# Causal masks from TensorE to GpSimd, 14 and 6 products of P V in a PSUM tile, and the last tokens of two batches in one output chunk, with a new written order

## The chip, the cores and the metric

The kernel runs on one core of a Trainium2 chip, as one launch. The metric is the device time of one execution in microseconds. The time before is the median of three runs.

## What is computed

Attention with a forget gate for 8 batches of 8 heads (576 tokens, head size 64), and then a gated FFN with a convolution of three taps over the tokens:

```python
scores = scale * np.matmul(q, k.transpose(0, 1, 3, 2))
cum = np.cumsum(np.log(np.clip(f, 0.0001, 1.0)), axis=-1)
scores = np.where(causal, -1e9, scores + cum[:, :, :, None] - cum[:, :, None, :])
attn = softmax(scores)                       # over the keys
x = np.matmul(attn, v)                       # heads side by side: 576 x 512 for each batch
h = np.maximum(x @ w_in, 0.0)                # 512 -> 1024
conv = sum of conv_w[k] * h shifted by k - 1 # along the tokens
out = (h * sigmoid(conv)) @ w_out            # 1024 -> 512
```

Inputs and output are float32; the matmuls run in 16-bit types.

## The kernel before

**Work.** The 64 heads go in 16 half batches `hb` of four heads. 576 tokens are four blocks of 128 and a tail of 64. Scores are made transposed, keys on the partitions. For each pair of heads `i` (two pairs in a half batch) `sd` makes the diagonal blocks, `so` the blocks off the diagonal (one step for each head), and `st` the tail's own 64 x 64 blocks for the half batch. `ed`, `eo` and `et` are ScalarE's exponentials of these. The decay is in the scores' matmul already, through two more rows of K and Q.

**The mask.** For half batches in `MASK_PE` a matmul with the identity (`masked`, L370) adds -1e30 above the diagonal before the scores are added, and ScalarE writes the result in 16 bits. For the others `ed` and `et` write float32 tiles (`pd`, `p3`, two of each), and GpSimd's `md` and `mt` (L406, L385) select from these into the 16-bit tiles. `signs`, the constants for the decay rows, lie in one of the `pd` tiles.

**P V and its normalization.** `pv` (L438) multiplies the exponentials by V with a column of ones, 65 columns for each head and block of queries, in three steps for a half batch: query blocks 0 and 1, blocks 2 and 3, the tail. Each takes one PSUM tile. `n` on VectorE takes the reciprocal of the sums (L445) and multiplies (L446). `t` and `tx` turn the result for the FFN.

**The FFN.** For each batch `b` and each 128 columns `ff` of 1024: `f` (L468) on PE, `r` (relu, L478) on ScalarE, `c` and `d` (the convolution, L483 and L485) on VectorE, `a` (tanh, L488) on ScalarE, `g` (the gate, L492) on VectorE. The second matmul `o` goes by chunks of 128 tokens over all `ff` (L499); the tail of 64 tokens goes by itself, in two halves of 256 columns (L503). `e` evicts from PSUM and `s` stores. In the last batch these go chunk by chunk as gates get ready.

**Loads.** SyncE (SP) issues them in order: `ld` (plain loads of Q and K for the first two half batches, transposed on PE by `tp`), `q` (transposing loads, L229), `v`, the weights `wi` and `wo`, and the decay rows `rw` and `fi`, which come from an image in memory that `ki` and `zc` write. `cl` writes Q and K from PSUM (L221, L223) or clamps them after the transposing load (L235); `va` casts V (L266, L268) and `wic` and `woc` cast the weights (L546).

**The order.** `ORDER` is a list of about a thousand steps, written by a search. Each engine issues its steps in the order of that list, and `@` names the engine where there is a choice. Four PSUM tiles `ps` of 1024 float32 columns and the other buffers are given out in that order too.

## Time and profile before

| | |
|---|---|
| median of three runs | 256.92 us (256.37 to 257.09) |
| span of the profiled execution | 254.4 us |
| PE (matmuls) busy | 235.6 us, 93% of the span |
| DVE (VectorE) busy | 216.8 us, 85% |
| ACT (ScalarE) busy | 217.4 us, 85% |
| POOL (GpSimd) busy | 45.9 us, 18% |
| moved by DMA | 48.24 MB, 190 GB/s in the mean |

The profiled execution's own time is not listed beside its span. The span goes from its first to its last instruction; the three runs' times hold what lies around that as well. Busy times are sums over the span; an engine with less busy time than another can still set the pace in one stage. The granted clock of TensorE is 0.999 of full speed in the mean.

### The profile page before, as it was taken

The numbers are of one execution on the slowest core, as the hardware profiler recorded it, in microseconds if no ns is written. First come the engines' busy times: TensorE is split into PE (matmuls) and PEld (weight loads), VectorE is DVE, ScalarE is ACT, GpSimd is POOL, SyncE is SP. The second block draws the span as 40 slices with busy tenths as digits, with TensorE's granted clock in tenths as the row PEclk, the third lists the DMA queues.
The fourth block names the chain that finished last, engine by engine and source line by source line (L and its number), as shares of the span: only waits on it lengthen the run. The fifth ranks groups of instructions, "written<-read, shape, count | busy, mean of one in ns | idle before, by whom it ended". The sixth has DMA issues, their size and how long they took to land.

```text
span 254.4 us, 6767 instructions
## 1 busy us (share of the span) xinstructions
PE 235.6 (93%) x2784; PEld 171.8 (68%) x2784; DVE 216.8 (85%) x353; ACT 217.4 (85%) x295; POOL 45.9 (18%) x79
## 2 busy tenths in 40 slices
...
GB/s 181 304 163 225 225 208 172 196 198 293 210 193 207 260 124 230 213 253 208 212 259 247 200 179 213 230 238 174 223 236 270 251 23 80 5 84 1 103 112 180
DMA packets 114695, 48.24 MB, mean 190 GB/s; under 512 B 104034, under 2 KB 105250, under 8 KB 114664
## 3 DMA queue, kind: packets, MB, share of 16 engines
...
q0 software_dynamic: 208, 0.51, 0.6%
...
## 4 chain that ended last, share of the span: by engine, by line
PE 57%; DVE 15%; DMA 9%; SPq 7%; ACT 5%; issue 4%; POOL 0%; DVEq 0%; POOLq 0%; ACTq 0%
PE ps L468 14%; PE ps L499 14%; PE ps L362 12%; PE ps L438 9%; DVE u L483 5%; DVE hg L492 4%; SPq L258 4%; DMA vf<-in_v_dram 4%; DVE u L485 3%; DMA hg<-in_k_dram 3%; PE ps L454 2%; PE ps L503 2%; DMA qk<-in_k_dram 2%; ACT pp L420 2%; PE ps L370 2%
## 5 line engine op out<-in xcount | busy, mean ns | idle before, releaser
L420 ACT ACTIVATE pp<-ps 128x1024 f16<-128x1024 f32 x64 | 65.0, 1038 | 6.6 <-PE ps L362 4.9
L468 PE MATMUL ps<-xt,w_in_f 128*128 128x288 f16 x512 | 68.9, 286 | 1.8 <-ACT xt L459 0.8
L362 PE MATMUL ps<-qk 128*128 128x128 bf16 (+2 forms) x576 | 63.6, 240 | 1.6 <-ACT ht L478 1.1
L499 PE MATMUL ps<-w_out_f,hg 128*128 128x512 f16 x256 | 59.9, 379 | 0.1
L468 PEld LDWEIGHTS <-w_in_f 128*128 128x128 f16 x512 | 48.8, 98 | 15.8 <-issue 2.5
L483 DVE SCALAR_TENSOR_TENSOR u<-ht,cwt 128x576 f32<-128x576 f16 x64 | 54.8, 862 | 2.8 <-ACT ht L478 2.8
L485 DVE SCALAR_TENSOR_TENSOR u<-ht,cwt,u 128x576 f32<-128x576 f16 x64 | 52.9, 831 | 1.7
L362 PEld LDWEIGHTS <-qk 128*128 128x128 bf16 x576 | 40.7, 98 | 17.6 <-issue 3.6
L488 ACT ACTIVATE hg<-u,cw 128x576 f16<-128x576 f32 x64 | 49.0, 786 | 1.8 <-DVE u L485 1.5
L492 DVE SCALAR_TENSOR_TENSOR hg<-hg,ht 128x576 f16<-128x576 f16 x64 | 49.6, 804 | 0.8 <-ACT hg L488 0.8
L478 ACT ACTIVATE ht<-ps 128x576 f16<-128x576 f32 x64 | 41.2, 667 | 5.4 <-PE ps L468 4.6
L499 PEld LDWEIGHTS <-hg 128*128 128x128 f16 x256 | 24.2, 98 | 25.4 <-DVE hg L492 0.8
L438 PE MATMUL ps<-va,pp 128*128 128x65 f16 x896 | 33.5, 193 | 4.0 <-POOL va L266 1.8
L438 PEld LDWEIGHTS <-pp 128*128 128x128 f16 x896 | 32.1, 97 | 6.2 <-issue 3.2
L406 POOL TENSOR_SCALAR_AFFINE_SELECT pp<-pd 128x1024 f16<-128x1024 f32 x16 | 19.4, 1215 | 63.9 <-ACT pd L403 60.8
L446 DVE TENSOR_TENSOR xm<-ps,rc 128x512 f16<-128x512 f32 (+1 forms) x48 | 28.9, 603 | 1.7
L509 ACT COPY ob<-ps 128x1024 f32<-128x1024 f32 (+1 forms) x21 | 16.8, 800 | 2.4 <-PE ps L503 1.0
L403 ACT ACTIVATE pd<-ps 128x1024 f32<-128x1024 f32 x16 | 16.6, 1036 | 1.0 <-PE ps L362 0.8
L403 ACT ACTIVATE pp<-ps 128x1024 f16<-128x1024 f32 x16 | 16.2, 1038 | 1.3 <-PE ps L362 1.3
L235 DVE TENSOR_SCALAR qk<-qk,lim 128x2304 uint16<-128x2304 uint16 x12 | 10.4, 875 | 7.3 <-DMA qk<-in_k_dram 4.9
L370 PE MATMUL ps<-mask,ident 128*128 128x512 bf16 (+1 forms) x40 | 14.3, 358 | 0.7 <-ACT ht L478 0.4
L445 DVE RECIPROCAL rc<-ps 128x8 f32<-128x8 f32 (+1 forms) x48 | 9.3, 193 | 5.9 <-PE ps L438 4.9
...
## 6 DMA issues: line engine op xcount, KB each, us to landing
...
out_dram<-ob SPq DMA_DIRECT2D x14, 512.0 KB, 3.1
...
ob<-in_moe_w_in_dram SPq DMA_DIRECT2D x4, 512.0 KB, 5.8
ob<-in_moe_w_out_dram SPq DMA_DIRECT2D x4, 512.0 KB, 6.4
...
```

What stands on the lines that cost most here:

```text
L362: nc.tensor.matmul(o, tk[:, h * S + k0:h * S + k0 + 128], tq[:, h * S + q0:h * S + q0 + n], start=first, stop=last and not by_matmul(hb, h))
L403: nc.scalar.activation(o, ps_of(f"sd{i}").rearrange("p (s c) -> p s c", s=2), AF.Exp, scale=SCALE)
L420: nc.scalar.activation(pair(i)[:, s, 512:1536], ps_of(f"so{i}.{s}"), AF.Exp, scale=SCALE)
L438: nc.tensor.matmul(o, block(hb, h, m, n), va[:, h, m, 0:D + 1], start=(m == 0), stop=(m == n))
L446: nc.vector.tensor_tensor(xm[:, 2 * u:2 * u + nj, :].rearrange("p j (h d) -> p j h d", d=D), got[:, :, :, 0:D], r.unsqueeze(3).broadcast_t ...
L468: nc.tensor.matmul(ps[:, MB + 288 * a:MB + 288 * (a + 1)], w_in_f16[:, cc, 128 * ff:128 * (ff + 1)], xt[:, cc, 288 * a:288 * (a + 1)], sta ...
L478: nc.scalar.activation(ht_of(b, ff)[:, 1:1 + S], ps_of(f"f{b}.{ff}")[:, MB:MB + S], AF.Relu, scale=0.5)
L483: nc.vector.scalar_tensor_tensor(u, ht[:, 0:S], cwt[:, ff, 0:1], ht[:, 1:1 + S], op0=ALU.mult, op1=ALU.add)
L485: nc.vector.scalar_tensor_tensor(u, ht[:, 2:2 + S], cwt[:, ff, 1:2], u, op0=ALU.mult, op1=ALU.add)
L488: nc.scalar.activation(hg_of(b, ff), u_t[slot[f"c{b}.{ff}", "u"]], AF.Tanh, scale=cw[:, ff, 1:2])
L492: nc.vector.scalar_tensor_tensor(hv, hv, 1.0, ht_of(b, ff)[:, 1:1 + S], op0=ALU.add, op1=ALU.mult)
L499: nc.tensor.matmul(ps[:, 512 * (c % 2):512 * (c % 2 + 1)], hg_of(b, ff)[:, 128 * c:128 * (c + 1)], w_out_f16[:, ff, :], **kw)
```

## The change

Four things change in the code, and the order is a new one.

- The mask of half batches 2 to 7 is GpSimd's, as that of 8 to 15 is already. `signs` gets a tile of its own, since the `pd` tiles are now used earlier.
- P V of a half batch goes into two PSUM tiles instead of three: the first holds 14 products (query blocks 0 to 2 and two heads of block 3), seven to a bank, the second the other 6. Normalization has two steps.
- A new step `k` copies the last 64 tokens of each batch's gated columns into a tile `tl` that two batches share, batch by batch, and `ff` by `ff` in the last one. The second matmul runs over these 128 tokens once for two batches, with all 512 columns.
- In the new order, 12 diagonal and 6 tail masks, 18 casts of V and all 8 weight casts are GpSimd's (before: 8 casts of V and 6 of the weights), `ki` is on GpSimd's queue instead of SP's, and evictions and casts are spread anew over ScalarE and VectorE.

The start of both orders, and the code:

```diff
-cw dca ld0 ld0.1.1 dcl dcs ld0.0.0 ld1 ld0.0.1 tp0.0.0 cl0.0.0@ACT cwt ld0.1.0 tp0.0.1 tp0.1.0 tp0.1.1 ld1.0.0 tp1.0.0
-dck cl0.0.1@ACT cl0.1.0@DVE cl0.1.1@ACT cl1.0.0@ACT ld1.0.1 tp1.0.1 q2.0 cl2.0 cl1.0.1@ACT sd0 ed0 tp1.1.0 tp1.1.1
-cl1.1.1@ACT ki@SP q2.1 sd1 so0.0 eo0.0 ed1 so1.1 eo1.1 so1.0 v0.0 v0.3 cl1.1.0@DVE rw1 so0.1 eo1.0 eo0.1 v0.4 v0.2
-v0.1 sd3 ed3 so3.0 sd2 eo3.0 ed2 cl2.1 wi0 rw2 wi1 wic1@POOL so2.1 va1.0@DVE eo2.1 st0 et0 va0.0@DVE va0.1@DVE pv0.0
-n0.0 so2.0 st1 et1 eo2.0 pv0.1 so3.1 pv0.2 eo3.1 va1.1@ACT sd5 q3.1 n0.1 n0.2 pv1.0 q3.0 wi3 n1.0 pv1.1 n1.1 pv1.2
-n1.2 ed5 so5.1 eo5.1 cl3.1 wic0@POOL t0 tx0@ACT t1 tx1@DVE cl3.0 wi2 wic3@POOL q5.0 sd4 ed4 rw3 so4.1 eo4.1 f0.0 r0.0
-f0.1 f0.2 f0.3 q5.1 v1.0 r0.1 v1.1 v1.2 v1.3 va2.0@POOL c0.0 d0.0 c0.1 wic2@ACT q4.1 r0.3 d0.1 so4.0 f0.4 c0.3 r0.2
-c0.2 d0.3 eo4.0 h0 sd7 sd6 so5.0 a0.0 g0.0 a0.1 g0.1 r0.4 ed7 c0.4 d0.4 so7.0 eo5.0 cl5.1 so7.1 ed6 f0.5 cl5.0 a0.4
...
+ld0 ld0.0.1 ld0.0.0 ld0.1.1 ld1 cw dca ld0.1.0 dcl dcs dck ld1.0.0 tp0.0.0 q3.1 tp0.0.1 cl0.0.0@ACT cl0.0.1@ACT
+tp0.1.0 tp0.1.1 v0.0 cl0.1.0@ACT ld1.0.1 sd0 q2.0 cl0.1.1@ACT cwt so0.0 st0 ki@POOL eo0.0 tp1.0.0 tp1.0.1 q3.0 ed0
+cl1.0.0@ACT et0 cl1.0.1@ACT v0.3 tp1.1.0 tp1.1.1 cl2.0 cl1.1.0@ACT sd1 v0.1 cl1.1.1@ACT so1.0 eo1.0 ed1 so1.1 so0.1
+eo0.1 rw1 sd2 so2.1 so2.0 v0.2 q2.1 eo1.1 v0.4 cl3.0 va0.0@DVE va0.1@POOL sd3 wi0 ed2 st1 ed3 cl3.1 so3.0 rw3
+va1.0@DVE et1 cl2.1 eo2.1 pv0.0 so3.1 eo3.0 eo2.0 pv0.1 sd7 va1.1@DVE eo3.1 n0.0 q4.0 sd6 n0.1 t0 tx0@DVE ed6 wi1 zc
+wic0@POOL rw2 pv1.0 st3 q4.1 et3 n1.0 so7.0 v1.0 ed7 pv1.1 md7 so6.0 eo7.0 so6.1 st2 wic1@POOL q5.0 n1.1 t1 eo6.0 v1.1
+et2 mt2 sd5 tx1@DVE sd4 md6 eo6.1 mt3 cl4.0 ed5 so5.0 v1.3 ed4 md5 f0.0 eo5.0 cl4.1 r0.0 f0.1 r0.1 f0.2 r0.2 so5.1
+f0.3 eo5.1 so4.0 c0.0 d0.0 h0 r0.3 so4.1 c0.2 rw4 d0.2 cl5.0 so7.1 v1.2 eo4.0 sd9 q5.1 md4 c0.1 so9.1 eo7.1 c0.3 eo4.1
+d0.3 va3.0@DVE v1.4 sd8 so8.1 d0.1 va2.0@POOL cl5.1 ed9 eo9.1 ed8 md8 wi3 a0.0 va2.1@POOL pv3.0 wi2 va3.1@ACT st4 et4
...
@@ -137,8 +137,8 @@
     NPL = 2
     PAIRS = 2
     NCL = 8
-    MASK_PE = (0, 1, 2, 3, 4, 5, 6, 7)
-    NPD, NP3 = 2, 2
+    MASK_PE = (0, 1)
+    NPD, NP3, NTL = 2, 2, 2
     VW = D + 2
     MB = 224
 
@@ -178,7 +178,9 @@
     pd_t = [cpool.tile([128, 2, 512], FP32, name=f"pd{t}") for t in range(NPD)]
     p3_t = [cpool.tile([128, HH, SL], FP32, name=f"p3{t}") for t in range(NP3)]
     xm_t = [cpool.tile([128, NKB, HH * D], FP16, name=f"xm{t}") for t in range(NX)]
-    rc_t = [cpool.tile([128, 2, HH], FP32, name=f"rc{t}") for t in range(NRC)]
+    rc_t = [cpool.tile([128, 2, 7], FP32, name=f"rc{t}") for t in range(NRC)]
+    tl_t = [cpool.tile([128, NFF, 128], FP16, name=f"tl{t}") for t in range(NTL)]
+    signs = cpool.tile([64, 2 * S], BF16, name="signs")
     xt_t = [cpool.tile([128, NCC, S], FP16, name=f"xt{t}") for t in range(NXT)]
     ht_t = [cpool.tile([128, S + 2], FP16, name=f"ht{t}") for t in range(NHT)]
     u_t = [cpool.tile([128, S], FP32, name=f"u{t}") for t in range(NU)]
@@ -190,7 +192,7 @@
     cwrow = pd_t[0].rearrange("p s c -> p (s c)")[0:3, 0:D_FF]
 
     plan = Plan({"ps": 4, "p": NP, "pt": NPT, "va": NVA, "vf": NVF, "xm": NX, "rc": NRC, "xt": NXT, "ht": NHT, "u": NU,
-                 "hg": NHG, "ob": NOB, "pd": NPD, "p3": NP3})
+                 "hg": NHG, "ob": NOB, "pd": NPD, "p3": NP3, "tl": NTL})
     slot = plan.slot
     add = plan.add
 
@@ -295,7 +297,6 @@
                             op0=ALU.is_equal, op1=ALU.mult)
     nc.vector.tensor_scalar(one3, hfx[0:3, 0:3], lit[0:3, 0:1], None, op0=ALU.is_equal)
 
-    signs = pd_t[1].rearrange("p s c -> p (s c)").bitcast(BF16)
     plus, minus = (signs[0:BH, x * S:(x + 1) * S] for x in range(2))
     nc.gpsimd.memset(plus, 1.0)
     nc.gpsimd.memset(minus, -1.0)
@@ -429,22 +430,25 @@
             c = 128 * m if m == n else OFF[m] + 128 * (n - m - 1)
         return p[:, c:c + 128]
 
+    SPLIT = (0, 14, HH * NKB)
+
     def pv(hb, u):
         ps, va = ps_of(f"pv{hb}.{u}"), va_t[slot[f"va{hb}.0", "va"]]
-        for j, n in enumerate(((0, 1), (2, 3), (4,))[u]):
-            for h in range(HH):
-                o = ps[:, 512 * j + (D + 1) * h:512 * j + (D + 1) * (h + 1)]
-                for m in range(n + 1):
-                    nc.tensor.matmul(o, block(hb, h, m, n), va[:, h, m, 0:D + 1], start=(m == 0), stop=(m == n))
+        for j in range(SPLIT[u + 1] - SPLIT[u]):
+            n, h = divmod(SPLIT[u] + j, HH)
+            c = 512 * (j // 7) + (D + 1) * (j % 7)
+            for m in range(n + 1):
+                nc.tensor.matmul(ps[:, c:c + D + 1], block(hb, h, m, n), va[:, h, m, 0:D + 1], start=(m == 0), stop=(m == n))
 
     def norm(hb, u):
         ps, rc, xm = ps_of(f"pv{hb}.{u}"), rc_t[slot[f"n{hb}.{u}", "rc"]], xm_t[slot[f"n{hb}.0", "xm"]]
-        nj = 2 if u < 2 else 1
-        got = ps.rearrange("p (j c) -> p j c", j=2)[:, 0:nj, 0:(D + 1) * HH].rearrange("p j (h c) -> p j h c", c=D + 1)
-        r = rc[:, 0:nj, :]
+        a, g = (2, 7) if u == 0 else (1, SPLIT[2] - SPLIT[1])
+        got = ps.rearrange("p (j c) -> p j c", j=2)[:, 0:a, 0:(D + 1) * g].rearrange("p j (h c) -> p j h c", c=D + 1)
+        r = rc[:, 0:a, 0:g]
         nc.vector.reciprocal(r, got[:, :, :, D])
-        nc.vector.tensor_tensor(xm[:, 2 * u:2 * u + nj, :].rearrange("p j (h d) -> p j h d", d=D), got[:, :, :, 0:D],
-                                r.unsqueeze(3).broadcast_to((128, nj, HH, D)), op=ALU.mult)
+        x = xm.rearrange("p n c -> p (n c)")[:, D * SPLIT[u]:D * SPLIT[u + 1]]
+        nc.vector.tensor_tensor(x.rearrange("p (j h d) -> p j h d", j=a, d=D), got[:, :, :, 0:D],
+                                r.unsqueeze(3).broadcast_to((128, a, g, D)), op=ALU.mult)
 
     def turn(hb):
         ps, xm = ps_of(f"t{hb}").bitcast(FP16), xm_t[slot[f"n{hb}.0", "xm"]]
@@ -491,26 +495,25 @@
         hv = hg_of(b, ff)
         nc.vector.scalar_tensor_tensor(hv, hv, 1.0, ht_of(b, ff)[:, 1:1 + S], op0=ALU.add, op1=ALU.mult)
 
+    def tails(b, ffs, e):
+        t = tl_t[slot[f"k{b & ~1}", "tl"]][:, ffs[0]:ffs[-1] + 1, SL * (b % 2):SL * (b % 2 + 1)]
+        i = hg_t[slot[f"h{b}", "hg"]][:, ffs[0]:ffs[-1] + 1, S - SL:S]
+        {"ACT": nc.scalar.copy, "POOL": nc.gpsimd.tensor_copy, "DVE": nc.vector.tensor_copy}[e](t, i)
+
     def ffn2(b, first, c, ffs):
         ps = ps_of(first)
         for ff in ffs:
-            kw = dict(start=(ff == 0), stop=(ff == NFF - 1))
-            if c < 4:
-                nc.tensor.matmul(ps[:, 512 * (c % 2):512 * (c % 2 + 1)], hg_of(b, ff)[:, 128 * c:128 * (c + 1)],
-                                 w_out_f16[:, ff, :], **kw)
-            else:
-                for a in range(2):
-                    nc.tensor.matmul(ps[64 * a:64 * (a + 1), 0:256], hg_of(b, ff)[:, 512:576],
-                                     w_out_f16[:, ff, 256 * a:256 * (a + 1)], skip_group_check=True, **kw)
+            w = hg_of(b, ff)[:, 128 * c:128 * (c + 1)] if c < 4 else tl_t[slot[f"k{b & ~1}", "tl"]][:, ff, :]
+            nc.tensor.matmul(ps[:, 512 * (c % 2):512 * (c % 2 + 1)], w, w_out_f16[:, ff, :],
+                             start=(ff == 0), stop=(ff == NFF - 1))
 
     def evac(name, first, c, e):
-        n = 1024 if c < 4 else 256
+        n = 1024 if c < 4 else 512
         ob = ob_t[slot[name, "ob"]].rearrange("p j c -> p (j c)")
         (nc.scalar.copy if e == "ACT" else nc.vector.tensor_copy)(ob[:, 0:n], ps_of(first)[:, 0:n])
 
     def evac_chunk(b, c, e):
-        n, j = 512 if c < 4 else 256, c % 2
-        o, i = ob_t[slot[f"e{b}.{c & ~1}", "ob"]][:, j, 0:n], ps_of(f"o{b}.{c & ~1}.0")[:, 512 * j:512 * j + n]
+        o, i = ob_t[slot[f"e{b}.{c & ~1}", "ob"]][:, c % 2, :], ps_of(f"o{b}.{c & ~1}.0")[:, 512 * (c % 2):512 * (c % 2 + 1)]
         (nc.scalar.copy if e == "ACT" else nc.vector.tensor_copy)(o, i)
 
     def store_chunk(b, c):
@@ -525,7 +528,7 @@
             nc.sync.dma_start(outf[r:r + 256, :].rearrange("(j p) c -> p j c", p=128), ob)
         else:
             for a in range(2):
-                nc.sync.dma_start(outf[r:r + SL, 256 * a:256 * (a + 1)], ob[64 * a:64 * (a + 1), 0, 0:256])
+                nc.sync.dma_start(outf[r - S * (1 - a):r - S * (1 - a) + SL, :], ob[64 * a:64 * (a + 1), 0, :])
 
 
     def stage(w, j):
@@ -625,14 +628,14 @@
                 add(f"eo{i}.{s}", "ACT", [f"so{i}.{s}"], lambda i=i, s=s: off_exp(i, s), give=[("ps", f"so{i}.{s}")])
         mk = "e" if hb in MASK_PE else "m"
         need = [f"{mk}d{2 * hb}", f"{mk}d{2 * hb + 1}", f"va{hb}.0"] + [f"eo{2 * hb + p}.{s}" for p in range(2) for s in range(2)]
-        for u in range(3):
-            add(f"pv{hb}.{u}", "PE", need + ([f"{mk}t{hb}", f"va{hb}.1"] if u == 2 else []), lambda hb=hb, u=u: pv(hb, u),
+        for u in range(2):
+            add(f"pv{hb}.{u}", "PE", need + ([f"{mk}t{hb}", f"va{hb}.1"] if u else []), lambda hb=hb, u=u: pv(hb, u),
                 take=["ps"], behind=[f"pv{hb}.{u - 1}"] if u else [],
-                give=[("p", f"sd{2 * hb}"), ("p", f"sd{2 * hb + 1}"), ("pt", f"et{hb}"), ("va", f"va{hb}.0")] if u == 2 else [])
+                give=[("p", f"sd{2 * hb}"), ("p", f"sd{2 * hb + 1}"), ("pt", f"et{hb}"), ("va", f"va{hb}.0")] if u else [])
             add(f"n{hb}.{u}", "DVE", [f"pv{hb}.{u}"], lambda hb=hb, u=u: norm(hb, u),
                 take=["rc"] + (["xm"] if u == 0 else []), give=[("ps", f"pv{hb}.{u}"), ("rc", f"n{hb}.{u}")],
                 behind=[f"n{hb}.{u - 1}"] if u else [])
-        add(f"t{hb}", "PE", [f"n{hb}.{u}" for u in range(3)], lambda hb=hb: turn(hb), take=["ps"], give=[("xm", f"n{hb}.0")])
+        add(f"t{hb}", "PE", [f"n{hb}.{u}" for u in range(2)], lambda hb=hb: turn(hb), take=["ps"], give=[("xm", f"n{hb}.0")])
         add(f"tx{hb}", "DVE/ACT", [f"t{hb}"], lambda e, hb=hb: turned(hb, e), take=["xt"] if hb % 2 == 0 else [],
             give=[("ps", f"t{hb}")], behind=[f"tx{hb - 1}"] if hb % 2 else [])
 
@@ -653,25 +656,33 @@
         wo = [f"woc{j}" for j in range(4)]
         if last:
             for ff in range(NFF):
+                add(f"k{b}.{ff}", "POOL/ACT/DVE", [f"g{b}.{ff}"], lambda e, b=b, ff=ff: tails(b, [ff], e),
+                    behind=[f"k{b - 1}"])
                 for c in range(NKB):
-                    add(f"o{b}.{c}.{ff}", "PE", [f"g{b}.{ff}"] + (wo if ff == 0 else []),
+                    add(f"o{b}.{c}.{ff}", "PE", ([f"g{b}.{ff}"] if c < 4 else [f"k{b - 1}", f"k{b}.{ff}"]) + (wo if ff == 0 else []),
                         lambda b=b, c=c, ff=ff: ffn2(b, f"o{b}.{c & ~1}.0", c, [ff]),
                         take=["ps"] if ff == 0 and c % 2 == 0 else [],
                         behind=[f"o{b}.{c}.{ff - 1}"] if ff else [f"o{b}.{c - 1}.0"] if c % 2 else [])
         else:
-            for c in range(5):
-                a = c // 2
-                first = f"o{b}.{2 * a}"
+            add(f"k{b}", "POOL/ACT/DVE", [f"g{b}.{ff}" for ff in range(NFF)], lambda e, b=b: tails(b, list(range(NFF)), e),
+                take=[] if b % 2 else ["tl"], behind=[f"k{b - 1}"] if b % 2 else [])
+            for c in range(4):
+                first = f"o{b}.{2 * (c // 2)}"
                 add(f"o{b}.{c}", "PE", [f"g{b}.{ff}" for ff in range(NFF)] + wo,
                     lambda b=b, c=c, first=first: ffn2(b, first, c, range(NFF)), take=["ps"] if c % 2 == 0 else [],
-                    behind=[f"o{b}.{c - 1}"] if c else [], give=[("hg", f"h{b}")] if c == 4 else [])
+                    behind=[f"o{b}.{c - 1}"] if c else [], give=[("hg", f"h{b}")] if c == 3 else [])
+                if c == 3:
+                    plan.tasks[f"o{b}.3"]["behind"].append(f"k{b}")
+            if b % 2:
+                add(f"o{b}.4", "PE", [f"k{b - 1}", f"k{b}"] + wo, lambda b=b: ffn2(b, f"o{b}.4", 4, range(NFF)), take=["ps"],
+                    give=[("tl", f"k{b - 1}")])
         if last:
             for c in range(NKB):
                 add(f"e{b}.{c}", "ACT/DVE", [f"o{b}.{c}.{NFF - 1}"], lambda e, b=b, c=c: evac_chunk(b, c, e),
                     take=["ob"] if c % 2 == 0 else [], behind=[f"e{b}.{c - 1}"] if c % 2 else [])
                 add(f"s{b}.{c}", "SP", [f"e{b}.{c}"], lambda b=b, c=c: store_chunk(b, c))
             continue
-        for a in range(3):
+        for a in range(2 + b % 2):
             first, made = f"o{b}.{2 * a}", f"o{b}.{min(2 * a + 1, 4)}"
             add(f"e{b}.{a}", "ACT/DVE", [made], lambda e, b=b, a=a, first=first: evac(f"e{b}.{a}", first, 2 * a, e),
                 take=["ob"], give=[("ps", first)])
```

89 lines of the change are left out of this document (44 added, 45 removed).

## The prediction

> **What bounds the kernel now.** I read the table by stage first, then the chain that ended last, then the groups of instructions, and last the order of time on single engines. The stages (columns: stage, its length, then busy time and count of PE, PEld, DVE, ACT, POOL, granted clock, DMA share, GB/s) were cut at the first convolution on VectorE (39.6 us) and at the end of the last gate (245.9 us):
>
> ```profile
> 39.60:64.00 24.40, 20.36 (x275) 15.22 (x274) 21.89 (x34) 22.09 (x31) 5.00 (x5) 1.00 0.96 211
> 64.00:208.00 144.00, 142.02 (x1705) 104.78 (x1703) 136.13 (x210) 135.90 (x189) 30.36 (x35) 1.00 1.03 214
> 208.00:245.90 37.90, 37.80 (x364) 24.07 (x362) 37.25 (x58) 29.30 (x44) 1.77 (x3) 1.00 0.17 61
> 245.90:254.40 8.50, 4.02 (x28) 1.71 (x28) 1.12 (x2) 1.66 (x3) 0.00 (x0) 0.96 0.44 149
> sum 254.40, PE 235.59 PEld 171.81 DVE 216.78 ACT 217.43 POOL 45.89; mean PE 47.12 PEld 34.36 DVE 43.35 ACT 43.49 POOL 9.18
> ```
>
> PE is idle for 2.0 of the 144 us in the middle, so PE sets the pace there. But VectorE is idle for only 7.9 us of the same stretch, 2.5 us before it and 0.65 us after it: 11.0 us between the first convolution and the last gate. In the stage from 208 us on VectorE has no room at all. So I keep the account on VectorE. The span is the start of its first convolution, plus its work, plus its idle time, plus the tail after the last gate: 39.6 + 195.3 + 11.0 + 8.5 = 254.4. A change that relieves PE alone can take back at most those 11.0 us. The chain says the same for the middle; it is PE's own instructions back to back there:
>
> ```profile
> 165.91 1.73 PE ps L499 x8
> ...
> 171.94 0.99 PE ps L503 x16
> ```
>
> Eight matmuls of 512 columns take 1.73 us, or 0.216 each; the last 64 tokens of one batch (16 matmuls of 256 columns) take 0.99 us.
>
> **What goes from PE.** The mask on PE is one matmul for each half of a diagonal tile and one for each tail:
>
> ```profile
> L370 PE MATMUL ps<-mask,ident x40: 269/379/379, 12.4 to 106.6; 128*128 128x512 bf16 x32, 128*128 128x256 bf16 x8
> ```
>
> Six of eight half batches lose theirs: 24 x 0.216 + 6 x 0.108 = 5.8 us (256 columns taken as half of 512). The last 64 tokens of two batches cost 2 x 0.99 = 1.98 us and will cost one chunk of 1.73: 0.25 less, four times, 1.0 us. In all PE loses 6.8 us, and P V has the same matmuls as before. From the middle stage PE's relief can reach the span only through VectorE's idle time. If VectorE's idle share fell everywhere to that of the last full stage (0.65 of 37.9 us, 1.7%), the 11.0 us would be 3.5. I take 5.6, a gain of 5.4; its ends are 0, where the idle time has other causes, and 7.5.
>
> **What VectorE loses and gets.** Its groups over the whole run, kept apart by shape (busy us, mean ns of one):
>
> ```profile
> L483 DVE SCALAR_TENSOR_TENSOR u<-ht,cwt 128x576 f32<-128x576 f16 x64 | 54.8, 862 | 2.8 <-ACT ht L478 2.8
> L485 DVE SCALAR_TENSOR_TENSOR u<-ht,cwt,u 128x576 f32<-128x576 f16 x64 | 52.9, 831 | 1.7
> L492 DVE SCALAR_TENSOR_TENSOR hg<-hg,ht 128x576 f16<-128x576 f16 x64 | 49.6, 804 | 0.8 <-ACT hg L488 0.8
> L446 DVE TENSOR_TENSOR xm<-ps,rc 128x512 f16<-128x512 f32 x32 | 22.1, 692 | 1.1
> L235 DVE TENSOR_SCALAR qk<-qk,lim 128x2304 uint16<-128x2304 uint16 x12 | 10.4, 875 | 7.3 <-DMA qk<-in_k_dram 4.9 <-DMA qk<-in_q_dram 2.4
> L446 DVE TENSOR_TENSOR xm<-ps,rc 128x256 f16<-128x256 f32 x16 | 6.8, 425 | 0.6
> L459 DVE COPY xt<-ps 128x1152 f16<-128x1152 f16 x9 | 6.6, 753 | 1.4 <-PE ps L454 1.2
> L445 DVE RECIPROCAL rc<-ps 128x8 f32<-128x8 f32 x32 | 6.5, 203 | 4.3 <-PE ps L438 3.4 <-ACT pp L420 0.8
> L266 DVE CAST va<-vf 128x1024 f16<-128x1024 f32 x8 | 5.5, 711 | 5.2 <-DMA vf<-in_v_dram 5.2
> ...
> L445 DVE RECIPROCAL rc<-ps 128x4 f32<-128x4 f32 x16 | 2.8, 175 | 1.6 <-PE ps L438 1.4
> ...
> L514 DVE COPY ob<-ps 128x512 f32<-128x512 f32 x1 | 0.7, 691 | 2.1 <-PE ps L499 2.1
> ```
>
> A half batch is normalized now in three steps: 2 x (203 + 692) + 175 + 425 = 2390 ns. Straight lines through the two sizes of each operation (1.04 ns an element + 158; 7 ns + 147) give the two new ones: 245 + 1092 and 189 + 558 = 2084 ns. That is 0.31 us less for each of the 14 half batches after the first convolution: -4.3. The written order also moves work. Counted from c0.0 on, VectorE has 3 large V casts instead of 6 (-2.1) and 6 clamps instead of 8 (-1.75), but 3 output evictions of 1024 columns, 2 of 512, and 3 of the 7 whole-batch copies of the last 64 tokens (512 elements) more. The trace has no such eviction on VectorE: between 0.75 (1152 elements of the half size) and 1.38 (twice 0.69), I take 1.1, as the 1.04 ns an element says; 3.3 us. The 512-column ones are 0.69 each, 1.4. The copies lie between 0.43 and 0.69; 0.55, 1.7. The sum is -4.3 - 2.1 - 1.75 + 3.3 + 1.4 + 1.7 = -1.7 us, with ends at -3.2 and -0.4. ScalarE loses eight casts of V, two of the weights and nine evictions and gets two prepared tiles of Q and K and a few copies. It is not the last to be ready in the stages above, and I give its relief nothing. The stores of the last 64 tokens become half as many with rows twice as long; with a DMA share of 0.17 where most of them run, they count as nothing.
>
> **What GpSimd gets, and VectorE pays.** This is the largest term that the change does not name. In 216 to 245 us GpSimd does nothing. There VectorE's three steps of the FFN take (mean of 12):
>
> ```profile
> L485 DVE SCALAR_TENSOR_TENSOR u<-ht,cwt,u 128x576 f32<-128x576 f16 x12 | 9.8, 818 | 0.4
> L483 DVE SCALAR_TENSOR_TENSOR u<-ht,cwt 128x576 f32<-128x576 f16 x12 | 9.7, 812 | 0.0
> L492 DVE SCALAR_TENSOR_TENSOR hg<-hg,ht 128x576 f16<-128x576 f16 x12 | 8.6, 751 | 0.0
> ```
>
> Over the whole run their means are 862, 831 and 804: (50 + 13 + 53) x 64 = 7.4 us more. One place shows why. GpSimd masks three tiles, and in the same microseconds three gates take 4.08 us where 2.1 is their time:
>
> ```profile
> 174.67 4.23 POOL L406 TENSOR_SCALAR_AFFINE_SELECT pp<-pd 128x1024 f16<-128x1024 f32 x3 [4.65 <-ACT pd L403]
> ```
> ```profile
> 175.42 4.08 DVE L492 SCALAR_TENSOR_TENSOR hg<-hg,ht 128x576 f16<-128x576 f16 x3
> ```
>
> GpSimd's work from 39.6 us on, in its large groups:
>
> ```profile
> L406 POOL TENSOR_SCALAR_AFFINE_SELECT pp<-pd 128x1024 f16<-128x1024 f32 x16 | 19.4, 1215 | 63.9 <-ACT pd L403 60.8 <-PE ps L362 3.1
> L266 POOL CAST va<-vf 128x1024 f16<-128x1024 f32 x4 | 4.4, 1101 | 25.4 <-DMA vf<-in_v_dram 25.4
> L385 POOL TENSOR_SCALAR_AFFINE_SELECT pt<-p 128x256 f16<-128x256 f32 x8 | 3.7, 469 | 25.1 <-ACT p L382 23.9 <-PE ps L362 1.2
> L546 POOL CAST w_out_f<-ob 128x1024 f16<-128x1024 f32 x3 | 3.3, 1115 | 7.6 <-DMA ob<-in_moe_w_out_dram 7.6
> L268 POOL CAST va<-vf 64x256 f16<-64x256 f32 x4 | 2.0, 501 | 15.9 <-PE ps L468 14.1 <-DMA vf<-in_v_dram 1.8
> ```
>
> These are 32.8 us, and VectorE loses 7.4 / 32.8 = 0.226 us for each. The Trainium skill (SBUF — State Buffer, Who interferes with whom) states that a VectorE instruction with two inputs in SBUF contends with a GpSimd instruction that reads SBUF, and that the second of them to issue is blocked for the whole of the other. The trace agrees at 175 us, where three gates lost 2.0 us to three masks. New on GpSimd after the first convolution, by the order: 9 of the 12 diagonal masks (10.9 us) and 4 of the 6 tail masks (1.9), 5 large and 4 small V casts (5.5 + 2.0), 2 weight casts (2.2), and copies of the last 64 tokens, one of 512 elements and five of 64 (taken as 0.8 + 5 x 0.4 = 2.8 from the 501 and 1101 ns rows): 25.3 us. At 0.226 that is +5.7 us for VectorE. The lower end is 0, if all of it falls beside the normalizations, which read PSUM; the upper is the rate at 175 us, 1.97 / 4.23 = 0.47, or 12.
>
> The masks add a wait as well. P V of half batches 2 to 7 needs GpSimd's tile 1.2 us after the exponential, and a cast ahead of it in GpSimd's queue adds 1.1; P V then holds back the PE queue behind it, scores and FFN alike. Half batches 8 to 15 run so today with PE idle 2.0 us in 144, so I price it at nothing and keep it as a rival.
>
> **The start.** Before, the first convolution and the weights that its matmul needs go so:
>
> ```profile
> 4.77 7.18 SPq L229 DMA_TRANSPOSE qk<-in_q_dram  x1
> ...
> 24.06 0.40 SPq L538 DMA_DIRECT2D ob<-in_moe_w_in_dram  x1
> ```
> ```profile
> 39.67 0.82 DVE L483 SCALAR_TENSOR_TENSOR u<-ht,cwt 128x576 f32<-128x576 f16 x1 [1.93 <-ACT ht L478]
> ```
> ```profile
> L229 SPq DMA_TRANSPOSE qk<-in_q_dram x14: 2701/4831/7182, 4.8 to 170.3; - x14
> L229 SPq DMA_TRANSPOSE qk<-in_k_dram x14: 1892/3197/5617, 13.9 to 183.1; - x14
> ```
> ```profile
> ob<-in_moe_w_in_dram SPq DMA_DIRECT2D x4, 512.0 KB, 5.8
> ```
>
> The second part of w_in (wi1) leaves SP's queue at 24.06, behind two transposing loads. In the new order five stand ahead of it, q3.1 first and then q2.0, q3.0, q2.1 and q4.0. That is three more at 4.0 (the mean of the two medians), 12 us; the three image writes go to GpSimd's queue, idle then, which takes about 2 off, and the V loads and decay rows ahead of wi1 are as many as before. So wi1 leaves at 34, lands 5.8 later, is cast by GpSimd (1.1), and the matmuls and the relu, which I take as 2, bring the first convolution to 42.9: +3.2. ScalarE points the same way, with 19 large exponentials ahead of f0.0 instead of 16 and all eight prepared Q and K tiles instead of six. The ends are +1 and +5.5.
>
> **The tail.** The last chunk of batch 7 has eight matmuls of 512 columns instead of pairs of 256 (0.99 / 8 = 0.124): 8 x 0.09 = 0.7; I take +0.5, with ends at -0.5 and +1.5, since the order of the last matmuls is new.
>
> **The sum.** +3.2 - 1.7 + 5.7 - 5.4 + 0.5 = +2.3 on 254.4: 256.7. The median of the three runs is 256.92, 2.5 above the span, and I leave that margin as it is: 259.2 us.
>
> **Rivals.** *PE's relief comes through.* For it: PE's idle 2.0 of 144 us, and masks that fall beside P V and its normalization, both off the shared inputs, cost nothing. Then collisions add 2, the start 1, and the idle time gives 6.5: +1 - 1.7 + 2 - 6.5 + 0.5 = -4.7, or 252.2 us. It decides if the three FFN steps of VectorE do not lengthen by more than 2 us in sum and the first convolution begins before 41. *They cancel*, within 0.3% (0.8 us, about what a measurement of this kernel can tell from no change). *GpSimd's queue becomes the wait*: a mask behind one cast in each of the six half batches, 6 x 1.1 = 6.6 us of PE's time not given back, of which the forecast's idle time can hide about a quarter, so 256.7 + 5 = 261.7, and 264.2 us; against it stands that GpSimd has 46 us of work now and some 75 then. *The full lock*: if every GpSimd microsecond stopped VectorE by the share of its time that the three FFN steps have, (54.8 + 52.9 + 49.6) / 216.8 = 0.73, the new 25.3 us would cost 18.5 instead of 5.7: 259.2 + 12.8 = 272.0 us. It is what the block of whole instructions in the Trainium skill's SBUF page would do at its worst; the 0.226 of this trace speaks against it.
>
> **Numbers.** Forecast 0.42, PE's relief 0.39, cancelling 0.08, GpSimd's queue 0.08, the full lock 0.03. That gives 0.39 faster, 0.08 the same, 0.53 slower. Alone, the forecast runs from 257.7 (the 0.8 us above the median) to 262.4 (GpSimd's new work at 0.35, midway between the two rates, costs 3.2 more). The whole range goes from 250.2, the relief with no collisions at all, to 264.2, the case of GpSimd's queue.
>
> **What would show it.** Right: FFN steps of VectorE at means near 890, 850 and 850 ns, the first convolution near 43 us, VectorE idle below 6 us from there to the last gate, no idle PE waiting for GpSimd. Wrong: FFN steps no longer than now, or a first convolution before 41 us; or, on the other side, PE waiting for masks by more than 5 us.

## The result, and the profile after

The changed kernel takes 271.56 us (median of 4 runs, 270.72 to 272.3). The kernel before, run beside it, takes 257.0 (256.37 to 257.1). The ratio is 1.0582, with a 95% interval of 1.0551 to 1.0613: slower by 14.6 us, where the prediction said 2.3 slower and at most 264.2 us in all.

The table by stage of the changed kernel, cut as before at the first convolution on VectorE (45.2 us) and at the end of the last gate (258.9); the columns are those of the prediction's first fence:

```profile
45.20:64.00 18.80, 15.46 (x243) 12.48 (x241) 17.92 (x24) 17.06 (x24) 7.57 (x10) 1.00 0.98 188
64.00:208.00 144.00, 127.83 (x1510) 92.40 (x1508) 140.91 (x181) 118.34 (x160) 53.96 (x47) 1.00 0.97 207
208.00:258.90 50.90, 50.51 (x446) 32.48 (x444) 50.23 (x73) 41.47 (x61) 8.37 (x8) 1.00 0.17 58
258.90:269.50 10.60, 4.50 (x21) 1.86 (x19) 1.38 (x2) 1.66 (x3) 0.46 (x3) 0.85 0.53 175
```

PE is now idle for 16.2 of the 144 us in the middle (2.0 before), VectorE for 3.1 (7.9 before). VectorE sets the pace there, and the shares of the chain that ended last name it too, PE before and VectorE now:

```profile
PE 57%; DVE 15%; DMA 9%; SPq 7%; ACT 5%; issue 4%; POOL 0%; DVEq 0%; POOLq 0%; ACTq 0%
```
```profile
DVE 48%; PE 22%; DMA 8%; issue 8%; ACT 7%; SPq 6%; DVEq 0%; ACTq 0%
```

In the prediction's account the span is 45.2 + 209.06 + 4.6 + 10.6 = 269.5. Against before that is +5.5 for the start, +13.9 for VectorE's work, -6.4 for its idle time and +2.0 for the tail: +15.1 us. VectorE's costliest groups from the first convolution to the last gate, apart by shape:

```profile
L487 DVE SCALAR_TENSOR_TENSOR u<-ht,cwt 128x576 f32<-128x576 f16 x64 | 58.9, 930 | 2.1 <-ACT ht L482 2.1
L489 DVE SCALAR_TENSOR_TENSOR u<-ht,cwt,u 128x576 f32<-128x576 f16 x64 | 58.6, 932 | 1.1
L496 DVE SCALAR_TENSOR_TENSOR hg<-hg,ht 128x576 f16<-128x576 f16 x64 | 54.5, 870 | 0.7 <-ACT hg L492 0.4
L450 DVE TENSOR_TENSOR xm<-ps,rc 128x896 f16<-128x896 f32 x14 | 15.3, 1092 | 0.5
L450 DVE TENSOR_TENSOR xm<-ps,rc 128x384 f16<-128x384 f32 x14 | 7.8, 558 | 0.5
L237 DVE TENSOR_SCALAR qk<-qk,lim 128x2304 uint16<-128x2304 uint16 x6 | 6.7, 1130 | 0.0
```

The three FFN steps (columns: busy us, mean ns) take 930, 932 and 870 ns. With GpSimd idle the same steps took 812, 818 and 751 in the kernel before, so 64 of each now cost 64 x (118 + 114 + 119) = 22.5 us too much. I call this the excess; before it was 7.4. The rise of 15.1 is all of VectorE's added work and more. The two normalizations came out at 1092 and 558 ns, the numbers of the prediction's straight lines. GpSimd in the same stretch:

```profile
L407 POOL TENSOR_SCALAR_AFFINE_SELECT pp<-pd 128x1024 f16<-128x1024 f32 x25 | 33.5, 1350 | 28.4 <-ACT pd L404 28.4
L268 POOL CAST va<-vf 128x1024 f16<-128x1024 f32 x9 | 11.5, 1277 | 14.0 <-DMA vf<-in_v_dram 14.0
L386 POOL TENSOR_SCALAR_AFFINE_SELECT pt<-p 128x256 f16<-128x256 f32 x12 | 8.9, 744 | 58.7 <-ACT p L383 58.7
L270 POOL CAST va<-vf 64x256 f16<-64x256 f32 x8 | 6.6, 825 | 2.3 <-DMA vf<-in_v_dram 2.3
L549 POOL CAST w_out_f<-ob 128x1024 f16<-128x1024 f32 x4 | 5.9, 1476 | 8.0 <-DMA ob<-in_moe_w_out_dram 8.0
```

The counts are those of the prediction, but every mean has grown: 1215 to 1350, 1101 to 1277, 469 to 744, 501 to 825, 1115 to 1476. GpSimd's instructions that read SBUF take 71.9 us in this stretch, 34.3 before. One place in the order of time on the two engines:

```profile
62.58 2.67 POOL L407 TENSOR_SCALAR_AFFINE_SELECT pp<-pd 128x1024 f16<-128x1024 f32 x2 [0.49 <-ACT pd L404]
```
```profile
61.97 3.89 DVE L496 SCALAR_TENSOR_TENSOR hg<-hg,ht 128x576 f16<-128x576 f16 x3
```

Three gates beside two masks take 3.89 us where 2.1 is their time, as in the prediction (2.09 at 256.79 us of this trace): 1.8 lost to 2.67 of GpSimd, 0.67 for each.

### The profile page after: what moved, and what is told of

Read it like the earlier page. It is cut to its first block, busy times and chain, and to the rows that moved or that the text cites. A ratio compares the mean times of both kernels' runs of the same rounds, so it can differ in the third digit from the quotient of the medians.

```text
span 269.5 us, 6502 instructions
## 1 busy us (share of the span) xinstructions
PE 232.2 (86%) x2658; PEld 166.5 (62%) x2658; DVE 230.8 (86%) x326; ACT 212.5 (79%) x283; POOL 90.7 (34%) x118
## 4 chain that ended last, share of the span: by engine, by line
DVE 48%; PE 22%; DMA 8%; issue 8%; ACT 7%; SPq 6%; DVEq 0%; ACTq 0%
DVE u L487 14%; DVE hg L496 12%; DVE u L489 12%; PE ps L472 6%; PE ps L507 6%; DVE xm L450 4%; PE ps L363 4%; SPq L231 4%; DMA qk<-image 3%; PE ps L441 3%; ACT hg L492 2%; ACT pp L421 2%; DMA hg<-in_k_dram 2%; DMA out_dram<-ob 2%; DVE qk L237 2%
## 5 line engine op out<-in xcount | busy, mean ns | idle before, releaser
L363 PE MATMUL ps<-qk 128*128 128x128 bf16 (+2 forms) x576 | 62.0, 241 | 15.3 <-DVE xm L450 6.3
L472 PE MATMUL ps<-xt,w_in_f 128*128 128x288 f16 x512 | 70.6, 289 | 4.6 <-ACT ht L482 1.8
L421 ACT ACTIVATE pp<-ps 128x1024 f16<-128x1024 f32 x64 | 64.6, 1033 | 6.0 <-PE ps L363 2.7
L472 PEld LDWEIGHTS <-w_in_f 128*128 128x128 f16 x512 | 49.8, 99 | 19.9 <-issue 6.0
L487 DVE SCALAR_TENSOR_TENSOR u<-ht,cwt 128x576 f32<-128x576 f16 x64 | 58.9, 930 | 2.1 <-ACT ht L482 2.1
L489 DVE SCALAR_TENSOR_TENSOR u<-ht,cwt,u 128x576 f32<-128x576 f16 x64 | 58.6, 932 | 1.1
L363 PEld LDWEIGHTS <-qk 128*128 128x128 bf16 x576 | 39.3, 98 | 29.8 <-issue 15.2
L496 DVE SCALAR_TENSOR_TENSOR hg<-hg,ht 128x576 f16<-128x576 f16 x64 | 54.5, 870 | 0.7 <-ACT hg L492 0.4
L407 POOL TENSOR_SCALAR_AFFINE_SELECT pp<-pd 128x1024 f16<-128x1024 f32 x28 | 37.3, 1341 | 29.6 <-ACT pd L404 29.6
L404 ACT ACTIVATE pd<-ps 128x1024 f32<-128x1024 f32 x28 | 28.7, 1037 | 2.3 <-PE ps L363 2.1
L386 POOL TENSOR_SCALAR_AFFINE_SELECT pt<-p 128x256 f16<-128x256 f32 x14 | 10.3, 734 | 59.8 <-ACT p L383 59.8
L450 DVE TENSOR_TENSOR xm<-ps,rc 128x896 f16<-128x896 f32 (+1 forms) x32 | 26.4, 825 | 1.1
L237 DVE TENSOR_SCALAR qk<-qk,lim 128x2304 uint16<-128x2304 uint16 x12 | 12.4, 1046 | 13.4 <-DMA qk<-in_q_dram 11.6
L268 POOL CAST va<-vf 128x1024 f16<-128x1024 f32 x9 | 11.5, 1277 | 14.0 <-DMA vf<-in_v_dram 14.0
L270 POOL CAST va<-vf 64x256 f16<-64x256 f32 x9 | 7.3, 808 | 23.0 <-DMA vf<-in_v_dram 23.0
```

Of the source, the lines that this page charges most:

```text
L363: nc.tensor.matmul(o, tk[:, h * S + k0:h * S + k0 + 128], tq[:, h * S + q0:h * S + q0 + n], start=first, stop=last and not by_matmul(hb, h))
L407: nc.gpsimd.affine_select(pair(i)[:, :, 0:512].rearrange("p s (m j) -> p s m j", j=128), pd_t[slot[f"ed{i}", "pd"]].rearrange("p s (m j) - ...
L421: nc.scalar.activation(pair(i)[:, s, 512:1536], ps_of(f"so{i}.{s}"), AF.Exp, scale=SCALE)
L450: nc.vector.tensor_tensor(x.rearrange("p (j h d) -> p j h d", j=a, d=D), got[:, :, :, 0:D], r.unsqueeze(3).broadcast_to((128, a, g, D)), o ...
L472: nc.tensor.matmul(ps[:, MB + 288 * a:MB + 288 * (a + 1)], w_in_f16[:, cc, 128 * ff:128 * (ff + 1)], xt[:, cc, 288 * a:288 * (a + 1)], sta ...
L487: nc.vector.scalar_tensor_tensor(u, ht[:, 0:S], cwt[:, ff, 0:1], ht[:, 1:1 + S], op0=ALU.mult, op1=ALU.add)
```

## The experiments

The theory: GpSimd's instructions that read SBUF and VectorE's FFN steps lengthen each other, and this excess is the loss. The rivals: the rearranged order itself (queues, start, tail), or GpSimd's masks and casts coming late for whoever waits. The account of all kernels, in us; work, idle time and GpSimd are taken between the first convolution and the last gate, ratios are to the kernel before, run beside each:

| kernel | start | VectorE work | of it excess | idle | tail | span | GpSimd | ratio, 95% |
|---|---|---|---|---|---|---|---|---|
| before | 39.7 | 195.16 | 7.4 | 11.0 | 8.6 | 254.4 | 37.1 | |
| after | 45.2 | 209.06 | 22.5 | 4.6 | 10.6 | 269.5 | 69.9 | 1.0582, 1.0551 to 1.0613 |
| e1_masks_pe | 45.1 | 203.60 | 18.4 | 5.2 | 9.2 | 263.1 | 57.1 | 1.0359, 1.0326 to 1.0392 |
| e2_casts_act | 49.3 | 200.73 | 15.7 | 19.6 | 11.1 | 280.7 | 46.2 | 1.1024, 1.0995 to 1.1053 |
| e3_both | 51.2 | 194.41 | 8.7 | 20.8 | 9.2 | 275.7 | 33.2 | 1.0871, 1.0837 to 1.0905 |
| e12_casts_dve | 48.8 | 210.26 | 13.6 | 13.9 | 9.8 | 282.7 | 46.4 | 1.1209, 1.1158 to 1.1259 |
| e4_masks_write | 45.2 | 194.67 | 8.6 | 8.5 | 10.8 | 259.1 | 52.4 | 1.0135, 1.009 to 1.0181 |
| e7_masks_write_wait | 45.5 | 192.49 | 7.1 | 8.6 | 10.8 | 257.4 | 53.5 | 1.0136, 1.0054 to 1.0217 |
| d3_burst_read | 39.1 | 206.95 | 17.9 | 7.3 | 8.3 | 261.7 | 78.7 | 1.0385, 1.0322 to 1.0447 |
| d4_burst_write | 37.4 | 196.87 | 7.3 | 10.4 | 8.3 | 253.0 | 62.0 | 1.0026, 0.9991 to 1.0061 |
| e5_old_masks | 39.3 | 198.62 | 9.6 | 13.9 | 8.5 | 260.4 | 56.2 | 1.0253, 1.0197 to 1.0309 |
| e8_old_pv | 38.5 | 192.38 | 6.9 | 15.2 | 8.4 | 254.5 | 38.2 | 1.0043, 1.0007 to 1.008 |
| e9_old_tails | 39.9 | 195.37 | 6.3 | 12.4 | 9.7 | 257.3 | 37.3 | 1.0104, 1.0055 to 1.0152 |
| e6_old_packing | 41.4 | 194.55 | 9.1 | 13.6 | 9.8 | 259.3 | 36.4 | 1.0197, 1.0145 to 1.0248 |
| e11_all_pe | 38.5 | 192.16 | 2.4 | 21.3 | 8.4 | 260.4 | 13.9 | 1.0384, 1.034 to 1.0428 |
| e10_late_wi1 | 40.8 | 194.59 | 5.9 | 11.7 | 8.4 | 255.5 | 36.4 | 1.0033, 0.9991 to 1.0076 |

**Masks or casts taken back from GpSimd in the changed kernel.** In e1 the masks of half batches 2 to 7 go back to PE; in e2 GpSimd's casts of V and w_out go to ScalarE, in e12 the same casts to VectorE; e3 is e1 and e2 together.

```diff
-MASK_PE = (0, 1)                       # e1, e3
+MASK_PE = (0, 1, 2, 3, 4, 5, 6, 7)     # md4 to md15, mt2 to mt7 leave the order
-va…@POOL (18), woc…@POOL (4)           # in the order
+va…@ACT, woc…@ACT                      # e2, e3; in e12 @DVE
```

> The changed kernel with the causal mask of half batches 2 to 7 back on PE; order and all else as changed. Theory (GpSimd's reads of SBUF stop VectorE's FFN steps: 22.5 us of excess over the undisturbed 812, 818 and 751 ns for 72 us of GpSimd work, 0.31 us each): about 17 us of GpSimd work after the first convolution go, so VectorE's steps lose 5 us of excess and the time falls to about 266 us; PE's 5.8 us more hide in PE's idle time. Rival (the new order is bad by itself, by its late first convolution and its waits): 271 to 276, with PE's masks added.

> The changed kernel with GpSimd's 18 casts of V and 4 casts of w_out on ScalarE; order and all else as changed. Theory of GpSimd's reads: about 24 us of GpSimd work go, VectorE's excess falls by 7 to 8 us, the time to about 264 us; ScalarE's 17 us more hide in its 55 us of idle time. Rival (the order by itself): 271 to 280, with ScalarE's work added.

> The changed kernel with both: masks of half batches 2 to 7 on PE, and GpSimd's V and w_out casts on ScalarE. GpSimd has then about 30 us of work after the first convolution, as in the kernel before. Theory of GpSimd's reads: VectorE's excess back near 8 us, the time 257 to 260 us (what stays is the late first convolution, 5.6 us, and the tail, 2 us, less the packing). Rival (the order by itself): 268 us or more.

> The changed kernel with GpSimd's 18 casts of V and 4 of w_out on VectorE itself, in the same places of the order (e2, with these on ScalarE, held up ScalarE's queue and told nothing of VectorE). VectorE gets 22 casts more, 9 x 0.69 + 9 x 0.28 + 4 x 0.69 = 11.5 us. Theory of GpSimd's reads: some 25 us less reading gives back 7 to 9 us of excess, so the time is 272 to 276 us. Rival (casts on GpSimd cost VectorE nothing, only masks do): 281 us or more.

e1 took 265.19 us, as expected. PE has its 5.8 us of mask matmuls back and the span is still 6.4 us shorter than after's: VectorE's work fell by 5.5, of which the excess is 4.1. e2 took 282.39 us and e3 278.22, both 18 us or more above what was expected. In e2 the work fell by 8.3, but the idle time rose by 15 and the start by 4. Its waits, VectorE's and then PE's (who waits for whom: us in total, how often, the longest):

```profile
DVE rc L447 <- PE ps L440: 12.9, 12, 4.9
```
```profile
PE ps L440 <- ACT va L267: 5.1, 2, 2.7
...
PE ps L506 <- ACT w_out_f L548: 4.3, 2, 2.6
```

The casts now stand in ScalarE's queue between its exponentials and come late: P V and the second matmul wait for them, and VectorE waits for P V (0.9 us in the changed kernel). That this is where the 15 us come from is argued and not shown: one cast waits 2.5 us for its load, and PE's mean granted clock is lower too, 0.956 against 0.988. In e12, at 284.76 us where 272 to 276 were expected, the casts wait in VectorE's queue instead (clock 0.959), with a similar result:

```profile
PE ps L506 <- DVE w_out_f L548: 6.3, 2, 3.9
```

The times of e2, e3 and e12 alone would fit the rivals (the order by itself; casts that cost VectorE nothing). The excess doesn't: it fell in all three, and the time was lost to idle time, a later start and, in e12, the casts' own 10 us on VectorE. As prices of the casts the three are misses: the casts were well placed on an engine that could wait. The excess can still be read: it falls by 4.1 without the new masks (e1), by 6.8 and 8.9 without the casts (e2, e12) and by 13.8 without both (e3), of the 15.1 that the change added. That gives masks 4 to 7 and casts 7 to 10, with the reservation that the order ran differently in each.

**Masks that write but do not read.** Both leave the causal mask out: GpSimd writes a constant into the tiles instead. In e7 the exponential also writes these tiles first, so that GpSimd's instruction waits as the mask did.

```diff
-        nc.gpsimd.affine_select(pt_t[...][:, :, SL:128], p3_t[...], ...)
+        nc.gpsimd.memset(pt_t[...][:, :, SL:128], 0.5)
-        nc.gpsimd.affine_select(pair(i)[:, :, 0:512]..., pd_t[...]..., ...)
+        nc.gpsimd.memset(pair(i)[:, :, 0:512], 0.5)
-        o = pair(i)[:, :, 0:512] if i // 2 in MASK_PE else pd_t[...]      # e7, the tails alike
+        o = pair(i)[:, :, 0:512]
```

> The changed kernel with every GpSimd mask (28 diagonal, 14 tails) replaced by a GpSimd memset of the same 16-bit tile: the causal mask is left out, GpSimd writes as much and stays about as busy, but reads no SBUF. Theory that GpSimd's reads are what stops VectorE: the excess of VectorE's steps falls from 22.5 to about 10 us (that of the casts) and the time to about 259 us. Rival (any GpSimd work at the same time slows VectorE): excess and time stay, 269 to 272. Rival (P V waits for the mask): since a memset need not wait for the exponential, the time falls while VectorE's excess stays.

> As e4, but the wait stays: ScalarE writes the exponentials straight into the 16-bit tiles, GpSimd's memset of the same tiles (28 diagonal, 14 tails) comes behind it as the mask did, and P V waits for the memset. The causal mask is left out. What differs from the changed kernel is only that GpSimd does not read SBUF there. Theory of GpSimd's reads: VectorE's excess near 9 us, as in e4, and the time 259 to 262 us. Rival (e4 gained by P V no longer waiting for the masks): the time goes back to 268 us or more.

They took 259.45 and 261.1 us. The groups of e7, VectorE's and then GpSimd's:

```profile
L484 DVE SCALAR_TENSOR_TENSOR u<-ht,cwt,u 128x576 f32<-128x576 f16 x64 | 55.9, 889 | 1.1
L482 DVE SCALAR_TENSOR_TENSOR u<-ht,cwt 128x576 f32<-128x576 f16 x64 | 52.1, 824 | 0.3 <-ACT ht L477 0.3
L491 DVE SCALAR_TENSOR_TENSOR hg<-hg,ht 128x576 f16<-128x576 f16 x64 | 48.6, 779 | 1.4 <-ACT hg L487 1.3
```
```profile
L405 POOL MEMSET pp<- 128x1024 f16 x28 | 27.4, 993 | 27.1 <-ACT pp L402 27.1
```

GpSimd still works 53.5 us and waits for the exponentials as before, and the excess is 7.1, that of the kernel before. Of the change's +15.1 us of span 12.1 have gone, and the +3.0 that stay are start +5.8, work -2.7, idle -2.4 and tail +2.2. The reads of the old masks (half batches 8 to 15) have gone too, so 12.1 is not the price of the new ones alone.

**The same collision in the kernel before, by dose.** 40 instructions for GpSimd, in the written order one behind each of 40 gates, though they wait for the weights' casts alone: in d3 they copy a row of the weights to an unused tile, in d4 they only write that tile.

```diff
+ add(f"x{x}", "POOL", [f"wic{j}" for j in range(4)], lambda: nc.gpsimd.tensor_copy(scr, w_in_f16[:, 0, 0:S]))   # d3
+ add(f"x{x}", "POOL", [f"wic{j}" for j in range(4)], lambda: nc.gpsimd.memset(scr, 0.0))                        # d4
```

> The kernel before with 40 added GpSimd copies of 128x576 16-bit elements from the weights to a scratch tile, one behind a gate each in GpSimd's queue; they wait for nothing and nothing waits for them (in d1 the relu's buffer waited for the copies). Theory of GpSimd's reads: some 25 us more of reading at 0.22 to 0.31 give 5.5 to 8 us more excess of VectorE's FFN steps, and the time grows by 4 to 8 us. Rival (the changed kernel lost by P V's waits for masks, not by reads): the time stays within 1.5 us.

> As d3 with 40 GpSimd memsets of the scratch tile in the same places: GpSimd is as busy but reads no SBUF. Theory of GpSimd's reads: the excess stays within 1 us of the 7.4 before and the time within 1.5 us of the kernel before. Rival (any GpSimd work beside VectorE slows it): as d3.

d3 took 264.28 us, d4 255.98. The groups of d3 and of d4, VectorE's first:

```profile
L487 DVE SCALAR_TENSOR_TENSOR u<-ht,cwt,u 128x576 f32<-128x576 f16 x64 | 59.0, 927 | 1.7
L485 DVE SCALAR_TENSOR_TENSOR u<-ht,cwt 128x576 f32<-128x576 f16 x64 | 56.2, 884 | 2.5 <-ACT ht L480 2.4
L494 DVE SCALAR_TENSOR_TENSOR hg<-hg,ht 128x576 f16<-128x576 f16 x64 | 52.6, 850 | 0.0
```
```profile
L642 POOL COPY scr<-w_in_f 128x576 f16<-128x576 f16 x40 | 39.4, 984 | 1.4
```
```profile
L487 DVE SCALAR_TENSOR_TENSOR u<-ht,cwt,u 128x576 f32<-128x576 f16 x64 | 55.7, 875 | 1.7
L485 DVE SCALAR_TENSOR_TENSOR u<-ht,cwt 128x576 f32<-128x576 f16 x64 | 54.3, 854 | 4.2 <-ACT ht L480 4.2
L494 DVE SCALAR_TENSOR_TENSOR hg<-hg,ht 128x576 f16<-128x576 f16 x64 | 47.2, 766 | 0.6 <-ACT hg L490 0.6
```
```profile
L642 POOL MEMSET scr<- 128x576 f16 x40 | 24.0, 601 | 1.3
```

Nobody waits for either, and the two differ in the read. The copies raise the excess by 10.5 us, above the 5.5 to 8 expected (GpSimd works 41.6 us more, where 25 were assumed: 0.25 for each), and the span by 7.3; VectorE's idle time hides 3.7. The 24 us of writing raise neither the excess nor the time; at 0.25 for each they would have cost 6 us. This shows the mechanism in the kernel before, with no other part of the change.

An earlier pair had the same aim, with tiles that ScalarE needs: 32 copies of relu's result (d1) or 32 writes to its buffer (d2).

```diff
+ nc.gpsimd.tensor_copy(scr, ht_of(b, ff)[:, 1:1 + S])   # d1, 32 times
+ nc.gpsimd.memset(ht_of(b, ff)[:, 1:1 + S], 0.0)        # d2, 32 times
```

> The kernel before with 32 added GpSimd copies of 128x576 16-bit elements from the relu's tile into a scratch tile that nobody reads, one behind every other gate; some 20 us of GpSimd work that reads SBUF. Theory: VectorE's three FFN steps lose 0.2 to 0.35 us for each of these microseconds, 4 to 7 us more excess, and the time grows by 3 to 7 us. Rival (the masks cost by P V's wait, not by the shared reads): nothing waits on these copies but the relu's buffer, so less than 1.5 us.

> The kernel before with 32 added GpSimd memsets of the same relu tile (128x576 16-bit elements, after its last reader) in the same places; as d1, but GpSimd writes and does not read. Theory of GpSimd's reads: VectorE's excess stays near 7 us and the time within 1.5 us of the kernel before. Rival (any GpSimd work beside VectorE slows it): as d1.

They took 267.56 us (ratio 1.0384, 1.0305 to 1.0463) and 266.15 (1.0332, 1.0245 to 1.0419); the intervals overlap. Both missed: 3 to 7 us more were expected of d1, and at most 1.5 of d2, whose time by itself fits the rival that any work of GpSimd costs. In d1 the excess rose to 15.6, but relu also waited 5.2 us for a copy to free its buffer, and by the edit d2's buffers wait for GpSimd as well. The pair tells nothing apart, and d3 and d4 took its place.

**The change's parts put into the kernel before, one by one.** e5 gives GpSimd the masks of half batches 2 to 7, with md and mt right behind their exponentials; e8 has only the new packing of P V, e9 only the shared chunk of the last 64 tokens, e6 both of these; e11 moves all masks to PE.

```diff
-MASK_PE = tuple(range(8))
+MASK_PE = (0, 1)               # e5;  e11: tuple(range(16)), no md, mt
-pv.0 pv.1 pv.2, n.0 n.1 n.2    # 8, 8, 4
+pv.0 pv.1, n.0 n.1             # 14, 6: e8, e6, in the places of the old 0 and 2
-o{b}.4 in each batch
+k{b}@ACT; o{b}.4 in odd batches only    # e9, e6; with their e and s
```

> The kernel before, its order kept, with only the masks of half batches 2 to 7 on GpSimd (each right behind its exponential; the constants' tile by itself). Theory of GpSimd's reads: 18 masks of 15 to 20 us at 0.23 to 0.31 cost VectorE 4 to 5 us; PE's 5.8 us less give back at most what VectorE's idle time held there: 256 to 260 us. Rival (masks are worth what they free on PE): 251 to 254 us.

> The kernel before, its order kept, with only the two packings: P V in two PSUM tiles of 14 and 6 products, and the last 64 tokens of two batches in one chunk (the copies on ScalarE); masks on PE as before. By the account on VectorE, the 16 shorter normalizations give 4 us and PE's tails 1 us, of which ScalarE's copies and the new wait of P V for the tail exponentials take back up to 2: 252.5 to 255 us. Rival (the packing costs, because the second P V step now needs a longer chain and a half batch holds PSUM longer): 257 us or more.

> The kernel before, its order kept, with only P V in two PSUM tiles of 14 and 6 products, in the places of the first and the third step. e6, both packings, was 5 us slower than before. Theory A (P V in larger steps costs: longer waits at the start and a PE gap of 2 us with the clock at half behind it): 258 to 260. Theory B (the tails cost: ScalarE's copies wait in its queue for the last gate): about 254, by 4 us less on VectorE.

> The kernel before, its order kept, with only the last 64 tokens of two batches in one chunk, the copies on ScalarE just ahead of the fourth chunk. Theory A (P V's larger steps cost): within 1 us of the kernel before. Theory B (the tails cost): 257 to 260 us, with VectorE or PE waiting for ScalarE's copies.

> The kernel before with the masks of half batches 8 to 15 on PE as well, order kept: GpSimd has no masks left. By the account, VectorE's excess falls from 7.4 to about 3 us, and PE, which is idle for 2 of 144 us, gets 8 x (4 x 0.216 + 0.108) = 7.8 us more: 257 to 262 us, as PE sets the pace there. Rival (VectorE's excess is what counts in the kernel before too): 251 to 254, which would be the best of all kernels here.

e5 took 262.97 us (260.01 to 264.58), slower than the 256 to 260 expected. Its excess rose only by 2.2 for 19.1 us more of GpSimd; the wait for a mask that I had priced at nothing is there as well (VectorE's wait for PE, and that of PE for GpSimd):

```profile
DVE rc L446 <- PE ps L439: 8.1, 8, 3.2
```
```profile
PE ps L439 <- POOL pt L386: 3.2, 1, 3.2
```

e8 took 256.99 us, between its two expectations (258 to 260, or about 254). It saves VectorE 2.8 us of work, and its idle time rises by 4.2, mostly here (4.9 us before):

```profile
DVE rc L445 <- PE ps L438: 8.2, 12, 1.4
```

A step of 14 begins when 14 products are done, no longer when 8 are. e9 took 258.78, in the range of one of its two expectations (257 to 260): work the same, idle +1.4 and tail +1.1. e6, at 260.61 us where 252.5 to 255 were expected, is both and a start 1.7 later. So in the old order none of the three parts is faster alone, and their sum (+6.0, +0.1, +2.9 us of span) is below the +15.1 of the change. e11, at 263.86, above the 257 to 262 expected, shows the other end: excess 2.4, VectorE's idle time 21.3, and PE with 142.27 of 144 us busy:

```profile
64.00:208.00 144.00, 142.27 (x1685) 103.33 (x1686) 126.08 (x201) 129.24 (x180) 9.93 (x13) 1.00 1.00 209
```

The masks of half batches 8 to 15, 23.2 of GpSimd's 37.1 us, are worth their collisions there: of the splits run in the old order, before's is the fastest.

**Where the loss lies, step by step.** In the traces a step of the FFN is met when a mask, cast or copy of GpSimd overlaps it in time. Before, 32 of the 192 steps are met and lose 7.6 us against their undisturbed 812, 818 and 751 ns; the other 160 lose nothing (-0.2). In the changed kernel 70 are met and lose 22.7 us, the other 122 nothing (-0.3). In e7, 28 steps lie beside writes alone and lose nothing (-0.1). For each microsecond in which a read of GpSimd and a step overlap, the loss is 0.48 us before, 0.42 after, 0.36 in d3 and 0.41 in e5. What differs is how much of GpSimd's reading lies beside the steps: 16.0 of 33.9 us before (47%), 24.1 of 52.7 in e5 (46%), 53.5 of 69.9 in the changed kernel (77%).

**The start.** In e10 wi1 leaves SP's queue later, the prediction's reason for the late start alone.

```diff
-… wi1 … wic1@POOL … q3.0
+… q3.0 wi1 wic1@POOL
```

> The kernel before with one load moved: the second part of w_in leaves SP's queue behind the transposing loads q3.1 and q3.0 instead of ahead of them, some 9 us later. Theory (the start of the first convolution passes into the time): it starts near 43 instead of 39.7 and the time is 2.5 to 3.5 us longer, 258 to 259. Rival (VectorE's 11 us of idle time later on take it up): within 1 us of the kernel before.

It took 257.29 us, where 258 to 259 and a start near 43 were expected. wi1 left at 32.14 instead of 24.06, and the first convolution began only 1.1 us later (40.8). The chain does pass through wi1 here: its cast ends at 38.78, and the convolution follows 2.0 later. The dose was too small to decide whether a late start passes into the time: the ratio of 1.0033 reaches from 0.9991 to 1.0076. But wi1 at 32 does not make the start 43. In the changed kernel wi1 leaves at 32.44 (L541), and the chain that ended last goes on to what stands behind it in SP's queue:

```profile
32.44 0.57 SPq L541
...
33.51 6.13 DMA qk<-image
39.64 0.05 issue
39.69 0.29 PE ps L363 x4
...
42.49 1.93 PE ps L472 x8
```

The decay rows of the next half batch land at 39.64, and PE's queue waits there with the scores (L363) and the FFN's first matmuls (L472) behind them. Those eight take 1.93 us, at half the clock (below). wi1 is nearly as late: its cast on GpSimd ends at 39.33. And the half clock isn't needed for the late start: in e1, e4 and e7 the clock is 1.00 in these microseconds, and the first convolution comes at 45.1, 45.2 and 45.5 all the same, there with ScalarE's exponentials ahead of its first relu on the chain. Several paths end nearly together, and which of them sets the start stays open.

## Why the prediction was wrong

The account, the direction and the mechanism held; the size did not. Of the 12.8 us between the forecast's 256.7 and the span of 269.5, the collisions are 9.4.

- **GpSimd's work, the step that failed.** The term was 25.3 us at 0.226: +5.7, at most 12. It measured +15.1. The amount is wrong because the durations were those of a GpSimd that meets VectorE seldom: the counts by the growth of the means (25 x 135, 12 x 275, 9 x 176, 8 x 324, 4 x 361 ns) are 12.3 us, and 25.3 + 12.3 is the 37.6 measured. The rate is 15.1 / 37.6 = 0.40 for each new microsecond: above the mean of before, 0.226, and inside the bound of 0.47, though the place shown above lost 0.67. The mean of 0.226 held because only 47% of GpSimd's reading lay beside the FFN steps; in the changed kernel 77% does, while the loss for each microsecond beside them is much the same (0.48 and 0.42). I took the mean as if the new work would meet VectorE as seldom as the old. d3 and d4 show that it is the read; e7, where some 28 us of reads stay (casts and copies), has 7.1 / 28 = 0.25.
- **The full lock** had 3 chances in 100 and the time nearest to what came, 272.0. That is partly luck: its price, 18.5 us for the new work, is above the 15.1, and a start and a tail that were too low made up for it. The rule in the Trainium skill (SBUF — State Buffer, Who interferes with whom) names the pair that collides, and says that a GpSimd instruction that only writes is not part of it. e7 and d4 agree: 28 steps beside writes alone lost nothing, and 24.0 us of added writes left the excess at 7.3.
- **VectorE's own work**, -1.7: without the excess it is 187.8 before, 186.6 after, 186.1 in e4 and 185.4 in e7, so -1.2, -1.7 and -2.4. Right. Not in it: the clamp of Q and K grew from 875 to 1130 ns, 6 x 0.26 = 1.5 us.
- **VectorE's idle time**, -5.4 to 5.6: it is 4.6. The number is right, but the reason only in part: in e7, where PE has the same relief and the excess is as before, the idle time is 8.6, so the relief is worth 2.4. The rest closed because VectorE became the bound. Between first convolution and last gate PE's busy time fell from 200.2 to 193.8, close to the predicted 6.8, and PE's idle time took it.
- **The start**, +3.2 with wi1 leaving at 34: +5.5, the upper end, though wi1 left at 32.44, earlier than that. Its cast ended at 39.33, which by e10's 2.0 us from cast to convolution gives about 41.3. The other 4 us are not in that term; ScalarE's exponentials, which the prediction named beside it without a price, stand on the chain in e1, e4 and e7. The cause stays open.
- **The tail**, +0.5, at most +1.5: +2.0. Besides the matmuls, the last evictions wait for an output buffer until a store of 4.25 us is through; the chain of after:

```profile
258.61 4.25 DMA out_dram<-ob
...
262.96 1.08 ACT ob L517 x2
```

- **GpSimd's queue as the wait**: no PE instruction waits for GpSimd in the changed kernel. In e5, with another order, it does. **PE's relief comes through** failed by its own condition: the FFN steps lengthened by 15, not 2.

What would show it: first convolution near 43 (45.2), idle below 6 (4.6), no PE waiting for GpSimd (none); FFN steps near 890, 850, 850 (930, 932, 870), off by 40, 82 and 20. Open stays how the excess divides between masks and casts beyond the 4 to 7 and 7 to 10 above, since every way to move the casts brought its own waits. That GpSimd's reads cost 0.12 each when added in e5 (2.2 / 19.1) and 0.40 in the change goes with what they lie beside: of e5's 18.8 new microseconds 8.1 lie beside FFN steps; of the change's 36.0, all do on balance (37.5 more).
